# One weight piece converted ahead of the first round, and the loads in another order

## The chip, the cores and the metric

The kernel runs on one core of a Trainium2 chip. The metric is the device time of one execution in microseconds. The engines are TensorE (PE), VectorE (DVE), ScalarE (ACT), GpSimd (POOL) and SyncE (SP). SP only issues DMAs here; ACT issues a few as well. The DMA engines themselves are shared by all queues.

## The reference

An attention block is followed by a feed-forward block. Attention has 8 batches of 8 heads, sequence 576, head dimension 64, in float32:

```
scores = q @ k.T / 8
scores = where(scores >= rowmax(scores) - tau, scores, -1e9)
attn   = exp(scores - rowmax) / (rowsum + 1e-9)
x      = attn @ v            # then heads side by side: 4608 tokens x 512
```

The feed-forward block takes x through `w_in` (512 x 1024), then `h * softmax(h)`, a layer norm scaled by `g_ln`, and `w_out` (1024 x 512). The two weight matrices come as 64-bit floats, so the kernel, which works in float32, has to convert them.

## The kernel before

**Rounds.** The program is written out by a Python loop over rounds (`rnd`), 144 of them (NS), each with one slot of attention. A slot is 128 rows of scores of two heads at once. In each round PE makes the scores (`scores`, L386), DVE takes the row maximum less tau (`maxes`, L407), ACT makes the threshold (`ramp`, L422) and the exponential (`exps`, L431). One round later POOL normalises (`normalise`, L438 to L441) and DVE transposes in blocks of 32 (`blocks`, L453). Two slots make a unit; after the second one, three or four DMAs on SP (`wT<-T`, L462 to L469) move the blocks to where PE needs them. Some three rounds on, PE multiplies by v (`attend_steps`, pv, L494) and ACT keeps the result (xh, L524). The slot numbers and rounds are the same: unit of slots 6 and 7 has its pv in round 10.

The feed-forward work of a block of 128 tokens lies between these: `ff_h` (L557) in two rounds, then maximum (L572), exponential (L581), product (L587), statistics, normalising (L623 on ACT, L628 on DVE), a swap by DMA (L639), a transpose (uT, L649), and `ff_o` (L662) in two rounds. The first `ff_h` is in round 11, the first `ff_o` in round 17.

**The weights.** There are 16 pieces (NW) of 128 x 512: eight of `w_in`, eight of `w_out`. Each is loaded as 512 KB of 64-bit values (`weight_load`, a tile `raw`) and turned into float32 by integer steps:

- `weight_a`: exponent (DVE L253, ACT L258) and mantissa bits (DVE L259)
- `weight_b`: low word and mantissa (DVE L273), sign and exponent (DVE L276)
- `weight_gain`, for `w_out` only: times the gain `gs` (ACT L292)
- `weight_c`: product of the two (POOL L286)
- `weight_d`, for `w_out` only: two DMAs on SP that copy the piece with its halves swapped (`w<-w`, L299)

In round r, piece r has its `weight_b` and piece r + 1 its `weight_a`; `weight_gain`, `weight_c` and `weight_d` of piece r follow in round r + 1. So piece 15 is done in round 16. Each raw piece takes a buffer that belongs to other tiles later: `xh2`, `xh3`, `uT`, `xh1` in turn. The load of piece x + 4 is issued on SP right after `weight_b(x)`, and waits until that is done with the buffer. Pieces 0 to 2 are loaded from ACT's queue.

**The start.** q and k of pair 0 are turned on PE (`turn`, L323), copied to SBUF by ACT and DVE (`keep`, L340 to L344; q is scaled by `scl`, which comes from tau), and pairs 1, 2, 3 follow in rounds 0, 2 and 4 (`whole_pair`). `constants` fills small tiles and makes `scl` from tau. `gains` turns `g_rows` into `gs` in round 3.

**Order.** All of it is in the order of the program on each engine. SP's DMAs too start in program order, so one that waits for a buffer holds up all behind it.

Of the kernel before, what the change touches and what calls it, by code (L numbers as in the profile page):

```python
# [8 lines left out]
F32 = mybir.dt.float32  # L9
I32 = mybir.dt.int32  # L10
U32 = mybir.dt.uint32
I64 = mybir.dt.int64
# [4 lines left out]
P = 128  # L17
# [3 lines left out]
def kernel(  # L21
# [27 lines left out]
    nc = tc.nc  # L49
# [4 lines left out]
    NP = H // 2  # L54
    NPAIR = B * NP
    NC = DFF // P
# [8 lines left out]
    work = ctx.enter_context(tc.tile_pool(name="work", bufs=2))  # L65
# [11 lines left out]
    zero = const.tile([P, 1], F32, name="zero")  # L77
    ntau = const.tile([P, 1], F32, name="ntau")
    scl = const.tile([P, 1], F32, name="scl")
    g_rows = work.tile([NC, P], F32, tag="V", bufs=1, name="g_rows")  # L80
    gs = const.tile([P, NC], F32, name="gs")
    lims = [const.tile([P, 1], F32, name=f"lim{x}") for x in range(2)]

    wide = w_in.dtype == I64
# [4 lines left out]
    NK = S // 64  # L89
# [37 lines left out]
    def load_pair(i, nm, queue=None):  # L127
        raw = loads.tile(
            [P, NK * D], F32, tag="ends" if i == NP - 1 else nm, bufs=BUFS["ends" if i == NP - 1 else nm], name=nm
        )  # L130
        whole_rows[i, nm] = raw.rearrange("p (m d) -> p m d", m=NK)
        (queue or nc.sync).dma_start(out=raw, in_=rows_of[nm][P * i : P * i + P])
# [10 lines left out]
    def load_v(b, hf, parts):  # L143
        d = halves.setdefault((b, hf), {})
        if 0 in parts:
            d["v"] = loads.tile([P, 4, NK, D], F32, tag="v", bufs=3, name="v")
        to = d["v"].rearrange("p h m d -> p h (m d)")
        rows = rows_of["v"][64 * (H * b + 4 * hf) :][0:256]
        for part in parts:
            nc.sync.dma_start(**(  # L150
                dict(
                    out=to.rearrange("p (e o) n -> p o e n", o=2)[:, 0],
                    in_=rows.rearrange("(e r) n -> r e n", e=2),
                ),
                dict(out=to[:, 1], in_=rows[64:192]),
                dict(out=to[ROWS[1], 3], in_=rows[0:64]),
                dict(out=to[ROWS[0], 3], in_=rows[192:256]),
            )[part])
# [66 lines left out]
    def piece(x):  # L225
        if x < 2 * NP:
            c, hf = divmod(x, 2)
            cols = slice(512 * hf, 512 * hf + 512)
            return w_in[P * c : P * c + P, cols], w1[:, c, cols], W_UNIT
        c = x - 2 * NP  # L230
        return w_out[P * c : P * c + P], w2[:, 2 * c], gs[:, c : c + 1]

    NW = 2 * NP + NC
    raws = {}

    def weight_load(x):
        raw = work.tile(
            [P, 512], I64 if wide else F32, tag=("xh2", "xh3", "uT", "xh1")[x % 4 if x < 15 else 0],
            bufs=1, name="raw"
        )  # L240
        queue = nc.scalar if x < 3 else nc.sync
        queue.dma_start(out=raw, in_=piece(x)[0])
        raws[x] = dict(raw=raw)

    def weight_a(x):
        if not wide:
            return
        d = raws[x]
        hi = d["raw"].bitcast(I32).rearrange("p (n two) -> p n two", two=2)[:, :, 1]
        d["em"] = e, m = [  # L250
            work.tile([P, 512], I32, tag=t, bufs=n, name="em") for t, n in (("ob", 2), ("xe", 1))
        ]
        nc.vector.tensor_scalar(  # L253
            out=e, in0=hi, scalar1=20, scalar2=0x7FF,
            op0=ALU.logical_shift_right, op1=ALU.bitwise_and,
        )

        nc.scalar.activation(out=e, in_=e, func=AF.Relu, bias=lims[x >= 2 * NP], scale=8388608.0)  # L258
        nc.vector.tensor_scalar(  # L259
            out=m, in0=hi, scalar1=0xFFFFF, scalar2=0x100000,  # L260
            op0=ALU.bitwise_and, op1=ALU.bitwise_or,
        )

    def weight_b(x):
        d = raws[x]
        _, dst, unit = piece(x)
        if not wide:
            nc.vector.tensor_scalar(out=dst, in0=d["raw"], scalar1=unit, scalar2=None, op0=ALU.mult)
            return
        words = d["raw"].bitcast(I32).rearrange("p (n two) -> p n two", two=2)  # L270
        lo, hi = words[:, :, 0], words[:, :, 1]
        e, m = d["em"]
        nc.vector.scalar_tensor_tensor(  # L273
            out=dst, in0=lo.bitcast(U32), scalar=2.0**-32, in1=m, op0=ALU.mult, op1=ALU.add
        )
        nc.vector.scalar_tensor_tensor(  # L276
            out=e, in0=hi, scalar=-(2**31), in1=e, op0=ALU.bitwise_and, op1=ALU.bitwise_or
        )

    def weight_c(x):  # L280
        d = raws.pop(x)
        if not wide:
            return
        _, dst, _ = piece(x)
        e, _ = d["em"]
        nc.gpsimd.tensor_tensor(out=dst, in0=dst, in1=e.bitcast(F32), op=ALU.mult)  # L286
# [22 lines left out]
    def pair(i):  # L309
        if i not in pairs:  # L310
            qT = heads.tile([P, S], F32, tag="qT", bufs=6, name="qT")
            pairs[i] = dict(
                qT=qT,
                kT=heads.tile([P, S], F32, tag="kT", name="kT"),
                qe=heads.tile([P, ST], F32, tag="qe", name="qe"),
            )
        return pairs[i]
# [18 lines left out]
    def keep(room, i, nm, ms, by_act):  # L336
        of = room[:, 0 : 64 * len(ms)].rearrange("p (m x a) -> p m a x", a=2, x=32)
        to = pair(i)[nm + "T"].rearrange("p (a m x) -> p m a x", a=2, m=NK)[:, ms[0] : ms[-1] + 1]
        if nm == "k":
            (nc.scalar.copy if by_act else nc.vector.tensor_copy)(out=to, in_=of)  # L340
        elif by_act:
            nc.scalar.activation(out=to, in_=of, func=AF.Copy, scale=scl)
        else:
            nc.vector.tensor_scalar(out=to, in0=of, scalar1=scl, scalar2=None, op0=ALU.mult)  # L344
# [385 lines left out]
    for i in range(2 * NP, NPAIR, 2):  # L730
        b, hf = divmod(i // 2, 2)
# [27 lines left out]
            )  # L759

    with tc.manual_schedule():
        nc.scalar.dma_start(out=tau_t, in_=tau.partition_broadcast(P))
        load_pair(0, "q")
        load_pair(0, "k", nc.scalar)
        weight_load(0)
        constants()
        for x in range(1, 3):
            weight_load(x)
        for i in range(1, NP):
            load_pair(i, "q")  # L770
            load_pair(i, "k")
        nc.sync.dma_start(out=g_rows, in_=g_ln.rearrange("(c p) -> c p", p=P))
        tags, tiles = zip(take("tp"), take("tp"))
        turn(tiles[0], 0, "k", range(NK))
        turn(tiles[1], 0, "q", range(4))
        keep(tiles[0], 0, "k", range(5), True)
        keep(tiles[0][:, 320:], 0, "k", range(5, NK), False)
        keep(tiles[1], 0, "q", range(2), True)
        keep(tiles[1][:, 128:], 0, "q", range(2, 4), False)


        pieces = {r: x for x, r in enumerate(range(16))}
        whole = {0: 1, 2: 2, 4: 3}
        for r, hf, parts in ((0, 0, (0,)), (1, 0, (1, 2, 3)), (3, 1, (0,)), (5, 1, (1, 2, 3))):
            load_at[r] = [lambda hf=hf, parts=parts: load_v(0, hf, parts)]

        ready = []
# [8 lines left out]
        while True:  # L796
# [33 lines left out]
            if more:  # L830
                room = 1
                if busy and quarter > 1 and preps and rnd + 4 < first_slot(preps[0][2]):
                    room = 0
                if room and preps and preps[0][0] <= rnd:
                    items = preps.pop(0)[1]
                scores(rnd, items)
                if rnd == 0:
                    turn(tiles[1][:, 256:], 0, "q", range(4, NK))
                    keep(tiles[1][:, 256:], 0, "q", range(4, NK), True)
                    pairs_free += tags  # L840
                idle = quarter == 0 and cur is None and (
                    prev is None or bool(pv_due) and pv_due[0][0] <= rnd
                )
                loose = idle and rnd > NW
                if loose:
                    keeps(rnd, 0)
                    keeps(rnd, 1)
                maxes(rnd, loose)
                ramp(rnd, 0)
                if rnd == 0:  # L850
                    weight_a(0)
                if not loose:
                    keeps(rnd, 0)
                    keeps(rnd, 1)
                ramp(rnd, 1)
                exps(rnd)
# [86 lines left out]
            if rnd in pieces:  # L943
                x = pieces[rnd]
                weight_b(x)
                for y in {0: (3, 4), 11: (), 12: (15,)}.get(x, (x + 4,)):
                    if y < len(pieces):
                        weight_load(y)
                if x + 1 < len(pieces):
                    weight_a(x + 1)  # L950
            if rnd - 1 in pieces:
                weight_d(pieces[rnd - 1])
# [37 lines left out]
```

## Time and profile before

| | |
|---|---|
| median of 3 runs | 861.9 us (860.43 to 862.63) |
| the profiled execution | 862.95 us, span 861.1 us |
| PE busy | 820.3 us, 95% of the span |
| DVE busy | 681.7 us, 79% |
| ACT busy | 571.5 us, 66% |
| POOL busy | 502.0 us, 58% |
| first PE matmul | 6.85 us |
| first L407 on DVE (round 0) | 11.96 us |
| L407 of rounds 5, 10, 11, 17 | 37.53, 62.27, 69.79, 104.79 us |
| DMA moved | 168.54 MB, mean 196 GB/s |

The span runs from the first to the last instruction in the profile; the execution's own time lies some 2 us above it. Busy time is the sum of an engine's instructions, whether or not something waits for them. A round's start is read from its first L407 on DVE.

### The profile page before, as it was taken

Reading aid. Unit: us, or ns where it says so; the run is one execution under the profiler, and the core shown is the slowest. Engines: PE = TensorE matmul, PEld = TensorE weight load, DVE = VectorE, ACT = ScalarE, POOL = GpSimd, SP = SyncE. Lnnn points to the kernel's source line nnn. Section 1 sums busy time; section 2 is a strip of 40 time slices with the busy share of each in tenths; the row PEclk is TensorE's granted clock in tenths of the full one; section 3 lists DMA queues with packets and bytes.
Section 4 is the critical chain, followed back from the end, with each engine's and each line's share of the span. In section 5 each row is a group of like instructions: output and inputs, shape, how many; then the busy total and the mean of one; then the engine's idle time right before and its main releaser. Section 6 shows DMA issues by size and latency. Waiting matters only on the chain.

```text
span 861.1 us, 36103 instructions
## 1 busy us (share of the span) xinstructions
PE 820.3 (95%) x15361; PEld 561.8 (65%) x15361; DVE 681.7 (79%) x1243; ACT 571.5 (66%) x1127; POOL 502.0 (58%) x944
## 2 busy tenths in 40 slices
PE   4769899899999999999999999999999999999997
PEld 3547576677677667777777775555555565556655
DVE  4998978878788888888788887888788888787361
ACT  5887867767677667777677767777777776775121
POOL 2887856656666656565656655565666665555120
PEclk9779999999999999999999999999999999999999
DMA  7999887988878878887878877888788787655312
GB/s 260 242 264 232 213 219 188 227 231 203 224 196 226 197 180 218 209 220 193 212 197 224 209 184 196 219 217 209 189 223 224 203 189 182 159 142 139 69 38 62
DMA packets 75584, 168.54 MB, mean 196 GB/s; under 512 B 11416, under 2 KB 32928, under 8 KB 75424
## 3 DMA queue, kind: packets, MB, share of 16 engines
q1 hardware_dynamic: 74560, 164.25, 75.8%
q8 instruction: 120, 1.97, 1.0%
q10 hardware_dynamic: 864, 2.00, 0.6%
q14 instruction: 40, 0.33, 0.1%
HBM read 46.14 MB, written 9.44 MB: 65 GB/s over the span
## 4 chain that ended last, share of the span: by engine, by line
PE 79%; DMA 7%; DVE 4%; ACT 3%; SPq 3%; issue 2%; POOL 1%; ACTq 0%; DVEq 0%
PE o_ps L662 26%; PE h_ps L557 22%; PE pv L494 14%; PE s_ps L386 14%; DMA wT<-T 5%; PE h_ps L547 3%; ACT w L422 1%; ACT w L431 1%; DVE w L407 1%; DVE T L453 1%; DMA v<-in_v_dram 1%; SPq L464 1%; DMA k<-in_k_dram 1%; DVE w L273 1%; DMA V<-u 0%
## 5 line engine op out<-in xcount | busy, mean ns | idle before, releaser
L662 PE MATMUL o_ps<-w,uT 64*64 64x256 f32 x4608 | 266.5, 376 | 1.7 <-ACT xh L524 0.6
L422 ACT ACTIVATE w<-s_ps,nth 128x576 f32<-128x576 f32 x280 | 196.7, 738 | 103.7 <-DVE nth L407 89.0
L407 DVE CUSTOM_DVE_ANT_0 w<-s_ps,tau_t 128x576 f32<-128x576 f32 x280 | 200.0, 751 | 79.2 <-PE s_ps L386 52.2
L662 PEld LDWEIGHTS o_ps<-w,uT 64*64 64x64 f32 x4608 | 192.3, 133 | 85.5 <-ACT xh L524 12.3
L441 POOL TENSOR_SCALAR w<-w,sm 128x576 f32<-128x576 f32 x288 | 222.6, 785 | 14.3
L453 DVE STREAM_TRANSPOSE T<-w 128x576 f32<-128x576 f32 x288 | 207.7, 755 | 21.5 <-POOL w L441 19.7
L431 ACT ACTIVATE w<-w,ntau 128x576 f32<-128x576 f32 x288 | 219.5, 766 | 0.0
L557 PE MATMUL h_ps<-w,xh 64*64 64x512 f32 x1856 | 217.1, 589 | 0.7 <-issue 0.7
L494 PEld LDWEIGHTS pv<-wT,v 64*64 64x64 f32 x5760 | 168.2, 137 | 46.5 <-issue 22.7
L386 PE MATMUL s_ps<-kT,qT 64*64 64x512 f32 (+1 forms) x2048 | 168.2, 413 | 14.5 <-ACT w L422 13.5
L494 PE MATMUL pv<-wT,v 64*64 64x128 f32 (+1 forms) x5760 | 172.7, 265 | 7.9 <-DMA wT<-T 6.9
L557 PEld LDWEIGHTS h_ps<-w,xh 64*64 64x64 f32 x1856 | 98.9, 133 | 97.3 <-issue 68.0
L438 POOL TENSOR_SCALAR sm<-sm 128x2 f32<-128x2 f32 x144 | 36.4, 253 | 199.1 <-ACT w L431 195.7
L439 POOL TENSOR_TENSOR sm<-sm,mone 128x2 f32<-128x2 f32 x144 | 108.3, 752 | 12.0
L386 PEld LDWEIGHTS s_ps<-kT,qT 64*64 64x64 f32 x2048 | 66.0, 136 | 24.4 <-ACT w L422 17.9
L524 ACT COPY xh<-pv 128x256 f32<-128x256 f32 x64 | 25.4, 397 | 78.9 <-PE pv L494 78.9
L623 ACT ACTIVATE V<-u,nb,rs 128x1024 f32<-128x1024 f32 x36 | 44.7, 1240 | 38.1 <-POOL nb L613 31.9
L649 DVE STREAM_TRANSPOSE uT<-V 128x1024 f32<-128x1024 f32 x36 | 44.2, 1229 | 18.7 <-DMA V<-u 18.6
L431 ACT ACTIVATION_READ_ACCUMULATOR w<-w,ntau 128x1 f32 x288 | 55.3, 192 | 0.0
L587 DVE TENSOR_TENSOR u<-h_ps,u 128x1024 f32<-128x1024 f32 x36 | 42.8, 1190 | 9.9 <-ACT u L581 9.9
L628 DVE TENSOR_SCALAR u<-u,rs,nb 128x1024 f32<-128x1024 f32 x36 | 34.6, 961 | 17.9 <-ACT V L623 17.9
L572 DVE TENSOR_REDUCE hm<-h_ps 128x1 f32<-128x1024 f32 x36 | 42.9, 1192 | 4.9 <-PE h_ps L547 2.7
(75 smaller groups left out, 559.3 us busy)
## 6 DMA issues: line engine op xcount, KB each, us to landing
wT<-T SPq DMA_DIRECT2D x160, 288.0 KB, 6.5
wT<-T SPq DMA_DIRECT2D x64, 576.0 KB, 5.9
v<-in_v_dram SPq DMA_DIRECT2D x16, 576.0 KB, 5.8
V<-u SPq DMA_DIRECT2D x144, 64.0 KB, 3.5
out_dram<-ob SPq DMA_DIRECT2D x71, 128.0 KB, 2.5
q<-in_q_dram SPq DMA_DIRECT2D x28, 288.0 KB, 6.0
k<-in_k_dram SPq DMA_DIRECT2D x27, 288.0 KB, 6.1
qT<-flip SPq DMA_DIRECT2D x48, 144.0 KB, 3.6
```

What stands on the lines that cost most here:

```text
L386: nc.tensor.matmul(out=ps[h][ROWS[y], ks], lhsT=lhsT, rhs=d["kT"][ROWS[h], ks], start=True, stop=True,)
L407: nc.vector.tensor_tensor_reduce(out=w, in0=ps[:, 0:S], in1=(zero if loose else tau_t).to_broadcast([P, S]), scale=1.0, scalar=BIG, op0=AL ...
L422: nc.scalar.activation(out=d["w"][x], in_=d["w"][x] if d["loose"] else d["ps"][x][:, 0:S], func=AF.Prelu, bias=d["nth"][x], scale=-1.0, al ...
L431: nc.scalar.activation(out=w, in_=w, func=AF.Exp, bias=ntau, scale=1.0, accum_out=sm[:, x : x + 1])
L439: nc.gpsimd.tensor_tensor(out=sm, in0=sm, in1=mone, op=ALU.pow)
L441: nc.gpsimd.tensor_scalar(out=w, in0=w, scalar1=sm[:, x : x + 1], scalar2=1.0, op0=ALU.mult, op1=ALU.mult)
L453: nc.vector.transpose(out=T[:, :, r, h, :], in_=w)
L494: nc.tensor.matmul(out=to, lhsT=d["v"][ROWS[u], (h0 + h - u) % 4, m,], rhs=rhs, start=m == 0, stop=m == NK - 1,)
L557: mm = nc.tensor.matmul(out=h[ROWS[y], f], lhsT=x[ROWS[r], c, ROWS[y]], rhs=w1_parts[ROWS[r], c, part ^ r], start=part == 0 and c == 0, st ...
L623: nc.scalar.activation(out=V, in_=u, func=AF.Identity, bias=nb, scale=rs)
L649: nc.vector.transpose(out=uT, in_=d["V"].rearrange("p y (m x) -> p m y x", x=32))
L662: nc.tensor.matmul(out=d["o"][ROWS[z], 512 * (r ^ other) : 512 * (r ^ other) + 256], lhsT=d["uT"][ROWS[r], m].rearrange("p y x -> p (y x)" ...
```

## The change

Piece 0 is loaded, converted and finished (`weight_a`, `weight_b`, `weight_c`) ahead of round 0, and round r then has `weight_b` of piece r + 1. All steps of pieces 1 to 15 so come one round earlier, and piece 15 is done in round 15. Raw pieces have six buffers instead of four (also `u` and `V`; `g_rows` moves from `V` to `xh0`). Six pieces are loaded ahead of round 0, the seventh behind `weight_b(0)`, and piece x + 6 behind `weight_b(x)`; piece 15 is asked for behind piece 12. ACT's queue keeps only k of pair 0 (now first) and tau; all other loads are on SP, in the order in which they are needed, with the first part of v among them. ACT alone makes the first copies of k and q.

```diff
-    g_rows = work.tile([NC, P], F32, tag="V", bufs=1, name="g_rows")
+    g_rows = work.tile([NC, P], F32, tag="xh0", bufs=1, name="g_rows")
...
-    def weight_load(x):
+    RAW = ['xh2', 'xh3', 'uT', 'xh1', 'u', 'V', 'xh2', 'xh3', 'uT', 'xh1', 'u', 'V', 'xh2', 'xh3', 'uT', 'xh2']
+    ASK = {0: [6], 1: [7], 2: [8], 3: [9], 4: [10], 5: [11], 6: [12], 7: [13], 8: [14], 12: [15]}
+
+    def weight_load(x, queue=None):
         raw = work.tile(
-            [P, 512], I64 if wide else F32, tag=("xh2", "xh3", "uT", "xh1")[x % 4 if x < 15 else 0],
+            [P, 512], I64 if wide else F32, tag=RAW[x],
             bufs=1, name="raw"
         )
-        queue = nc.scalar if x < 3 else nc.sync
-        queue.dma_start(out=raw, in_=piece(x)[0])
+        (queue or nc.sync).dma_start(out=raw, in_=piece(x)[0])
...
     with tc.manual_schedule():
+        load_pair(0, "k", nc.scalar)
         nc.scalar.dma_start(out=tau_t, in_=tau.partition_broadcast(P))
-        load_pair(0, "q")
-        load_pair(0, "k", nc.scalar)
-        weight_load(0)
+        load_pair(0, "q", nc.sync)
+        weight_load(0, nc.sync)
+        load_pair(1, "k", nc.sync)
+        load_pair(1, "q", nc.sync)
+        weight_load(1, nc.sync)
+        load_pair(2, "k", nc.sync)
+        load_pair(2, "q", nc.sync)
+        weight_load(2, nc.sync)
+        weight_load(3, nc.sync)
+        load_pair(3, "k", nc.sync)
+        load_pair(3, "q", nc.sync)
+        nc.sync.dma_start(out=g_rows, in_=g_ln.rearrange("(c p) -> c p", p=P))
+        weight_load(4, nc.sync)
+        load_v(0, 0, (0,))
+        weight_load(5, nc.sync)
         constants()
-        for x in range(1, 3):
-            weight_load(x)
-        for i in range(1, NP):
-            load_pair(i, "q")
-            load_pair(i, "k")
-        nc.sync.dma_start(out=g_rows, in_=g_ln.rearrange("(c p) -> c p", p=P))
         tags, tiles = zip(take("tp"), take("tp"))
         turn(tiles[0], 0, "k", range(NK))
         turn(tiles[1], 0, "q", range(4))
-        keep(tiles[0], 0, "k", range(5), True)
-        keep(tiles[0][:, 320:], 0, "k", range(5, NK), False)
-        keep(tiles[1], 0, "q", range(2), True)
-        keep(tiles[1][:, 128:], 0, "q", range(2, 4), False)
-        pieces = {r: x for x, r in enumerate(range(16))}
+        keep(tiles[0], 0, "k", range(NK), True)
+        keep(tiles[1], 0, "q", range(4), True)
+        weight_a(0)
+        weight_b(0)
+        weight_c(0)
+        weight_load(6)
+        pieces = {r: x for r, x in enumerate(range(1, NW))}
         whole = {0: 1, 2: 2, 4: 3}
-        for r, hf, parts in ((0, 0, (0,)), (1, 0, (1, 2, 3)), (3, 1, (0,)), (5, 1, (1, 2, 3))):
+        for r, hf, parts in ((1, 0, (1, 2, 3)), (3, 1, (0,)), (5, 1, (1, 2, 3))):
             load_at[r] = [lambda hf=hf, parts=parts: load_v(0, hf, parts)]
...
                 if rnd == 0:
-                    weight_a(0)
+                    weight_a(1)
...
                 weight_b(x)
-                for y in {0: (3, 4), 11: (), 12: (15,)}.get(x, (x + 4,)):
-                    if y < len(pieces):
-                        weight_load(y)
-                if x + 1 < len(pieces):
+                for y in ASK.get(x, ()):
+                    weight_load(y)
+                if x + 1 < NW:
                     weight_a(x + 1)
```

## The prediction

> **What bounds the kernel now.** I read the page's 40 slices first, to see where TensorE is not full.
>
> ```profile
> PE   4769899899999999999999999999999999999997
> ...
> DVE  4998978878788888888788887888788888787361
> ...
> PEclk9779999999999999999999999999999999999999
> DMA  7999887988878878887878877888788787655312
> ```
>
> A slice is 21.5 us. TensorE (PE) is full from about the fourth slice on; DVE and the DMA engines are full in the second and third, where PE is not and its clock is cut. The change touches the start and rounds 0 to 16 (to about 105 us), so I asked for busy time by stretch (columns: window, length, busy PE, PEld, DVE, ACT, POOL, PE clock, DMA share, GB/s).
>
> ```profile
> 40.00:50.00 10.00, 6.50 (x112) 4.50 (x108) 9.90 (x21) 7.70 (x16) 8.42 (x11) 0.83 1.03 253
> ...
> 60.00:70.00 10.00, 7.72 (x125) 5.96 (x123) 7.43 (x16) 6.65 (x16) 8.67 (x12) 0.74 0.99 259
> ...
> 200.00:400.00 200.00, 198.72 (x3825) 147.42 (x3820) 167.21 (x304) 139.63 (x277) 121.66 (x235) 1.00 0.83 209
> ```
>
> From 20 to 60 us DVE is busy 9.9 of 10 us: it sets the length of rounds 2 to 9, together with DMA engines that have no spare time. From 200 us on PE is busy 99% of the time. The later rounds are the same instructions in both kernels, so I take it that what is won or lost by round 18 stands at the end. Then the chain that ended last, in order of time (start, length, what), at the start and around 60 us:
>
> ```profile
> 1.17 5.55 DMA k<-in_k_dram
> ...
> 6.85 3.05 PE tp L323 x52
> ...
> 10.35 1.59 PE s_ps L386 x15
> ```
> ```profile
> 56.49 8.61 DMA wT<-T
> 65.10 0.04 issue
> 65.14 3.68 PE pv L494 x65
> ```
>
> The kernel starts when the first k lands (6.72). In round 10 PE waits for the turned attention weights of slots 6 and 7, 8.6 us after the issue of their last third. DVE's own timeline (start, length, instruction, idle time before it) shows what that costs:
>
> ```profile
> 66.95 0.41 DVE L259 TENSOR_SCALAR em<-raw 128x512 int32<-128x512 int32 x1
> 69.79 0.76 DVE L407 CUSTOM_DVE_ANT_0 w<-s_ps,tau_t 128x576 f32<-128x576 f32 x1 [2.43 <-PE s_ps L386]
> ```
>
> DVE had finished round 10 at 67.36 and could begin round 11 only at 69.79. Why does the transfer take 8.6 us? The queue ahead of it is full, though it stood empty earlier. The DMA view of the first 25 us (slices of 0.625 us):
>
> ```profile
> DMA  0037448799999999999999970069989930017499
> GB/s 0 0 29 96 162 100 137 273 413 390 426 403 434 387 417 414 398 401 422 383 394 417 406 262 0 0 79 269 236 291 359 402 144 4 0 26 79 157 334 249
> ```
>
> From 5 to 15 us the engines move about 405 GB/s. From 15 to 25 they move 1.64 MB, which at that rate is 4.1 us: 5.9 us of transfer time are lost, because piece 4 waits for piece 0's buffer and everything on SP waits behind it (issue 15.43).
>
> **The change, part by part.**
>
> *Start.* k goes first on ACT's queue, ahead of tau, as the first q does on SP's. That q, issued at 0.72, landed 4.2 us later, at 4.9: one bound for k. The other: k and q share the engines, and 0.59 MB are through at 5.2 by the GB/s row, 5.6 with the same lag to the landing. I take 5.3 between them: PE starts 1.4 us earlier (1.1 to 1.8). [...]
>
> [...]
>
> *All first copies on ACT.* k takes about 0.7 us on ACT (rows of 128x576: 0.63 to 0.72), q about 0.45. k's 36 matmuls end 2.2 us after the landing, q's 16 at 3.05, so q is in place at 3.55; before, ACT's half was done at 3.45 and DVE's at 3.83. No difference.
>
> *Piece 0 ahead of round 0.* Its bytes are the first 1.11 MB: 6.5 us by the row, landed near 7. Four DVE instructions (0.42, 0.42, 0.69, 0.68), one on ACT (L258, 0.72), one on POOL (L286, 1.29). DVE does the first three by 8.5; ACT's step stands behind its copies of k and q, 9.0 to 9.7; DVE's fourth ends at 10.4. Round 0's scores end near 10.6, when DVE can start L407 (before: 11.96). So it is covered by DVE's wait for the first scores, with 0.2 us to spare on DVE and 1.4 us on the landing. Without that cover each us late is a us of start.
>
> *Rounds 0 to 9.* Each still holds one piece's DVE work, so their length stays. The gain multiplication on ACT (L292, 0.71) begins in round 8 instead of 9, where ACT waits 0.47 for DVE: 0 to 0.2 us, taken as nothing.
>
> *Loads.* Before the first wT transfer (issued 25.5 before, 24 now) the queue now carries nine pieces instead of six: 1.57 MB or 3.9 us more, into the 5.9 us that were lost. Between there and the wT of slots 6 and 7 both kernels load six pieces, the same v and three wT sets. If only the bytes count, that wT lands 2.0 us earlier, at 63.1. If the queue is drained when the first wT comes (8.26 MB at 405 GB/s end at 24.1), nothing stands ahead of it any more, and each later set is limited by its own issue: last third issued at 56.49 - 1.4 = 55.1, plus the 5.9 to 6.5 us that wT takes over the whole run, 61.3. I take the middle, 62.2, since no row decides. [...]
>
> *Round 10.* PE is ready at 62.4 - 1.4 = 61.0 and waits until 62.2; pv starts 2.9 us earlier than 65.14, round 11 at 66.9. DVE alone would allow 67.36 - 1.4 = 65.96. So the start's 1.4 us are inside these 2.9, not on top (bounds 2.0 and 3.8).
>
> *Rounds 14 to 16* lose the piece that moved: L253 and L259 in 14, L273 and L276 in 15, L292 and L286 in 16. On the path is ACT's L258 at 92.74, behind which L623 starts at 93.37, while its other input (POOL, nb) ends at 92.76: 0.6 us (0.5 to 1.2, since L292 at 99.27 is also in the chain).
>
> *The last w_out swap* leaves SP one round earlier. PE waits for it once:
>
> ```profile
> 112.19 0.86 PE L662 MATMUL o_ps<-w,uT 64*64 64x256 f32 x10 [0.50 <-DMA w<-w]
> ```
>
> 0.5 us (0 to 1.4: SP issues the next wT 0.9 us late there, behind these loads). Late next: PE itself.
>
> Sum: 2.9 + 0.6 + 0.5 = 4.0 us. The profiled execution took 862.95 (span 861.1), so 858.95; the median, 861.9, becomes 857.9.
>
> **Rivals.**
>
> *The saturated queue swallows it.* For: DMA share 1.0 from 30 to 70 us; any byte put ahead is paid later. Then the wT of slots 6 and 7 lands at 65.1 still, the earlier start is waited away in round 10, and only 0.6 + 0.5 remain: 860.8. Against: the idle time from 15 to 25.
>
> *Slower: three more pieces stand ahead of wT.* If the time from 15 to 25 cannot be won back (piece 4 and v, 1.1 MB, took 5.6 us from issue to landing at an idle queue), the wT of slots 6 and 7 lands later by three pieces: 3.9 us at 405 GB/s, 6.0 at the 263 GB/s seen at 65 us. Round 11 starts that much later, less 1.1: 864.7 to 866.8. It decides against the change once that wT lands after 65.1 + 1.1 + 2.6 = 68.8.
>
> *PE's clock recovers.* pv of slots 6 and 7 took 3.73 us, that of slots 8 and 9 (at 77.42) 2.23; the granted clock is 0.74 from 60 to 70 and 1.00 after. Without the stall pv may run at full clock, 1.5 us shorter; with the landing at 61.3, DVE then bounds round 11 (3.8), and with the upper bounds of the rest (1.2, 1.4): 855.5. [...]
>
> **How the numbers follow.** My forecast (own range 855.5 to 859.3) has 0.47, the clock case 0.10, the swallowed gain 0.22, slower 0.18; 0.03 is for no effect. A measurement of this kernel tells 0.3% (2.6 us) from no change, so faster needs under 859.3: 0.57; same, with the swallowed gain and no effect: 0.25; slower 0.18. The range runs from 854.5, a little below the clock case, to 862.0, over the swallowed gain; most of the slower case is left out.
>
> **What would show it.** Right: first PE matmul near 5.4; first L407 near 10.6; no empty DMA slices between 5 and 23 us; the wait before round 11's L407 under 1 us; L662's wait for w<-w gone. Wrong: wT of slots 6 and 7 landing after 64, or DVE waiting for raw pieces (L253 idle on a DMA).

## The result and the profile after

The changed kernel took 856.97 us (median of 13 runs, 855.38 to 862.38) against 862.29 us before (13 runs, 857.14 to 868.88). The ratio is 0.9946 [0.9927, 0.9966], so 4.7 us less (2.9 to 6.3). The profiled execution took 856.02 us, span 854.0 us; its forecast was 858.95. In the experiments below, two executions lay far outside all others and are left out of the numbers (3023.6 us of e1, its profiled one, and 1435.7 us of the kernel before, beside e1 to e4).

The page's 40 slices of the changed kernel (a slice is now 21.35 us):

```profile
PE   5669899999999999999999999999999999999997
...
DVE  5999868889788888888788878888888888787361
...
PEclk9789999999999999999999999999999999999999
DMA  8998797898888788897878778888788877655212
```

DVE and the DMA engines are busier in the first slice, and PE's row is much as it was. Busy time by stretch says more (window, length, busy PE, PEld, DVE, ACT, POOL, PE clock, DMA share, GB/s):

```profile
40.00:50.00 10.00, 6.50 (x108) 4.52 (x104) 9.91 (x21) 7.70 (x16) 8.29 (x10) 0.83 1.01 274
60.00:70.00 10.00, 7.52 (x138) 5.47 (x136) 9.90 (x21) 8.59 (x19) 9.35 (x13) 1.00 0.76 186
200.00:400.00 200.00, 198.52 (x3828) 148.60 (x3824) 166.40 (x302) 139.50 (x278) 122.46 (x238) 1.00 0.85 210
```

From 60 to 70 us DVE is now busy 9.90 us instead of 7.43, PE's clock is 1.00 instead of 0.74, and the DMA share is 0.76 instead of 0.99. From 200 us on little differs. The first 25 us of the DMA view show the new order of the loads:

```profile
DMA  0037799974379999999999999999999999893999
GB/s 0 0 26 85 229 398 436 275 164 79 88 266 406 431 423 402 406 423 434 406 419 381 388 421 382 397 384 406 399 397 413 418 413 413 321 170 118 269 369 397
```

The empty stretch from 15 to 25 us is gone; a dip at 5 to 7 us (79 GB/s) is new, and one at 22 us (118 GB/s) is left. Around round 11, PE first and then DVE (start, length, instruction, idle time before it):

```profile
61.88 0.44 PE L496 MATMUL pv<-wT,v 64*64 64x128 f32 x4 [1.63 <-DMA wT<-T]
63.17 2.07 PE L496 MATMUL pv<-wT,v 64*64 64x128 f32 x66 [0.85 <-DMA wT<-T]
```
```profile
66.48 0.41 DVE L261 TENSOR_SCALAR em<-raw 128x512 int32<-128x512 int32 x1
66.82 0.74 DVE L409 CUSTOM_DVE_ANT_0 w<-s_ps,tau_t 128x576 f32<-128x576 f32 x1
```

PE still waits for wT of slots 6 and 7, which landed at 63.12. But the 66 multiplications then took 2.07 us, and DVE went from round 10 to round 11 without idle time. At the start the chain no longer begins with k:

```profile
1.17 6.89 DMA tau_t<-in_tau_dram
...
8.09 0.16 DVE scl L205
...
8.34 0.48 ACT qT L344
...
8.87 2.20 PE s_ps L388 x16
```

k landed at 4.83, earlier than either bound; tau landed at 8.07, and q's copy, which needs `scl`, waited 0.52 us for it. The wait of `ff_o` for the last swapped piece is gone: PE's timeline has its 64 multiplications in one piece.

```profile
104.29 3.71 PE L664 MATMUL o_ps<-w,uT 64*64 64x256 f32 x64
```

Of the 6.93 us between the two profiled executions, 3.85 are there when round 29 starts (163.86 against 167.71). Most of the rest belongs to this execution of the kernel before: its round 30 came 7.35 us after round 29, with a wait that the changed kernel's profile lacks (there, 4.44 us). DVE's timeline of the kernel before:

```profile
175.06 0.76 DVE L407 CUSTOM_DVE_ANT_0 w<-s_ps,tau_t 128x576 f32<-128x576 f32 x1 [2.83 <-PE s_ps L386]
```

### The profile page after: what moved, and what is told of

The parts are those of the page before. It is cut to its first block, busy times and chain, and to the rows that moved or that the text cites. A ratio compares the mean times of both kernels' runs of the same rounds, so it can differ in the third digit from the quotient of the medians.

```text
span 854.0 us, 36100 instructions
## 1 busy us (share of the span) xinstructions
PE 817.5 (96%) x15361; PEld 572.4 (67%) x15361; DVE 681.0 (80%) x1241; ACT 571.4 (67%) x1127; POOL 500.9 (59%) x944
## 4 chain that ended last, share of the span: by engine, by line
PE 79%; DMA 7%; DVE 4%; ACT 3%; POOL 3%; issue 2%; SPq 1%; ACTq 0%; DVEq 0%; POOLq 0%
PE o_ps L664 27%; PE h_ps L559 21%; PE s_ps L388 14%; PE pv L496 14%; DMA wT<-T 4%; PE h_ps L549 3%; ACT w L433 1%; ACT w L424 1%; DVE T L455 1%; DVE w L409 1%; POOL w L443 1%; DMA tau_t<-in_tau_dram 1%; DMA v<-in_v_dram 1%; DMA q<-in_q_dram 1%; POOL sm L441 1%
## 5 line engine op out<-in xcount | busy, mean ns | idle before, releaser
L409 DVE CUSTOM_DVE_ANT_0 w<-s_ps,tau_t 128x576 f32<-128x576 f32 x280 | 199.9, 750 | 72.0 <-PE s_ps L388 47.3
L664 PEld LDWEIGHTS o_ps<-w,uT 64*64 64x64 f32 x4608 | 201.3, 133 | 75.9 <-ACT xh L526 12.6
L496 PEld LDWEIGHTS pv<-wT,v 64*64 64x64 f32 x5760 | 165.6, 135 | 42.4 <-issue 21.2
L388 PE MATMUL s_ps<-kT,qT 64*64 64x64 f32 (+1 forms) x2048 | 168.2, 413 | 15.5 <-ACT w L424 12.9
L496 PE MATMUL pv<-wT,v 64*64 64x128 f32 (+1 forms) x5760 | 169.7, 261 | 5.5 <-DMA wT<-T 4.9
L559 PEld LDWEIGHTS h_ps<-w,xh 64*64 64x64 f32 x1856 | 101.8, 133 | 94.4 <-issue 63.1
L583 ACT ACTIVATE u<-h_ps,hm 128x1024 f32<-128x1024 f32 x36 | 40.2, 1116 | 10.4 <-DMA V<-u 5.7
```

Of the source, the lines that this page charges most:

```text
L388: nc.tensor.matmul(out=ps[h][ROWS[y], ks], lhsT=lhsT, rhs=d["kT"][ROWS[h], ks], start=True, stop=True,)
L409: nc.vector.tensor_tensor_reduce(out=w, in0=ps[:, 0:S], in1=(zero if loose else tau_t).to_broadcast([P, S]), scale=1.0, scalar=BIG, op0=AL ...
L496: nc.tensor.matmul(out=to, lhsT=d["v"][ROWS[u], (h0 + h - u) % 4, m,], rhs=rhs, start=m == 0, stop=m == NK - 1,)
L559: mm = nc.tensor.matmul(out=h[ROWS[y], f], lhsT=x[ROWS[r], c, ROWS[y]], rhs=w1_parts[ROWS[r], c, part ^ r], start=part == 0 and c == 0, st ...
L664: nc.tensor.matmul(out=d["o"][ROWS[z], 512 * (r ^ other) : 512 * (r ^ other) + 256], lhsT=d["uT"][ROWS[r], m].rearrange("p y x -> p (y x)" ...
```

## The experiments

**Theories.** Mine: the loads fill the empty stretch, wT of slots 6 and 7 lands earlier, and this is most of the gain; the conversion one round ahead is worth about 1 us; a still earlier start would be waited away at round 11. Rivals: the conversion does most of it; six buffers matter; the pair of profiles only caught one good and one bad execution. Edits are to the changed kernel. The ratios are to the kernel before, run beside each one.

The table gives the first L407 or L409 of some rounds in each profile (us), then the execution's time less the start of round 29. The two rows of means average three profiles of before and two of the changed kernel; each other row is one profile.

| kernel | round 0 | 11 | 19 | 29 | rest | ratio to before |
|---|---|---|---|---|---|---|
| before, mean | 12.29 | 69.66 | 117.97 | 169.49 | 692.8 | 1 |
| changed, mean | 11.13 | 67.46 | 112.11 | 165.18 | 691.9 | 0.9946, 0.9942 |
| e7 loads only | 10.17 | 67.24 | 115.04 | 166.76 | 691.7 | 0.9959 (e1) |
| e2 conversion only | 12.77 | 69.08 | 113.85 | 166.10 | 692.7 | 0.9947 |
| e3 four buffers | 10.76 | 66.29 | 112.70 | 164.92 | 692.5 | 0.9929 |
| e8 tau on POOL | 11.17 | 66.97 | 111.29 | 163.65 | 694.9 | 0.9928 |
| e9 swaps late | 10.62 | 66.02 | 115.17 | 167.25 | 693.6 | 0.9969 |
| e10 tau alone | 10.05 | 65.51 | 109.67 | 162.04 | 693.4 | 0.9938 |
| e11 late loads | 11.05 | 68.59 | 115.51 | 168.06 | 692.1 | 0.9983 |
| e12 late loads, tau alone | 10.03 | 67.34 | 113.28 | 165.47 | 692.4 | 0.9958 |

The rest lies between 690.9 and 694.9 us in all profiles but the first of before (695.2), whatever the variant. So what the change wins is won by round 29, and some 4 us vary from execution to execution behind it.

**The loads alone (e1, e7).** Piece 0 is converted inside round 0 again; loads and buffers stay as changed.

```diff
-        weight_a(0)
-        weight_b(0)
-        weight_c(0)
-        weight_load(6)
-        pieces = {r: x for r, x in enumerate(range(1, NW))}
+        pieces = {r: x for r, x in enumerate(range(NW))}
...
-                    weight_a(1)
+                    weight_a(0)
```

> The changed kernel with piece 0 converted inside round 0 again (piece r in round r, as before), but with the new order of the loads and the six buffers. Queue theory (the gain is made by the DMA queue: the wT transfer of slots 6 and 7 lands earlier): round 11 starts near 66.8 us as in the changed kernel, some 3 us earlier than before; then the 0.6 us of rounds 14 to 16 and the 0.5 us of the w<-w wait are missing: about 858 to 859.5 us. Conversion theory (the gain is made by taking one piece's work out of the rounds): nothing of it is left, 861 to 862.5 us.

Measured: 859.64 us, ratio 0.9959 [0.9936, 0.9981], 3.5 us less than before. The profile read here is e7, the same program:

> The loads-only kernel once more, for a profile of an ordinary execution. Queue theory: round 11 near 66.8 us, as in the changed kernel; rounds 14 to 17 without the 0.6 us, and PE waits 0.5 us for w<-w again. Conversion theory: round 11 at 69 us or later.

Measured: 858.44 us. Round 11 begins at 67.24, as early as in the changed kernel, and the wait for the swapped piece is back (PE's timeline):

```profile
111.36 0.86 PE L664 MATMUL o_ps<-w,uT 64*64 64x256 f32 x10 [2.23 <-DMA w<-w]
```

So the new order of the loads brings round 11 forward without the conversion. It need not be the bytes in the empty stretch that do it. Round 0 began 2.1 us ahead of the mean of before (k landed sooner, so PE began at 4.81 us instead of 6.85, and the scores took 1.21 us instead of 1.59), round 11 2.4 us. SP could issue the last third of wT of slots 6 and 7 that much earlier; the chain of e7 has it as

```profile
54.70 7.83 DMA wT<-T
```

In the three profiles of before it was issued at 56.49, 56.42 and 57.73 and took 8.61, 7.44 and 8.18 us. The earlier issue is most of the earlier landing, and 7.83 us lie among the times of before.

**The conversion alone (e2).** Loads, order and four buffers as before, piece 0 ahead of round 0:

```diff
-    RAW = ['xh2', 'xh3', 'uT', 'xh1', 'u', 'V', 'xh2', 'xh3', 'uT', 'xh1', 'u', 'V', 'xh2', 'xh3', 'uT', 'xh2']
-    ASK = {0: [6], 1: [7], 2: [8], 3: [9], 4: [10], 5: [11], 6: [12], 7: [13], 8: [14], 12: [15]}
+    RAW = ['xh2', 'xh3', 'uT', 'xh1'] * 3 + ['xh2', 'xh3', 'uT', 'xh2']
+    ASK = {**{x: [x + 4] for x in range(1, 11)}, 12: [15]}
...
```

The loads ahead of round 0 are again those of before, in its order and on its queues, except that piece 3 is loaded with them and piece 4 is asked for ahead of round 0. ACT alone still makes the first copies.

> The changed kernel's conversion (piece 0 ahead of round 0, piece r + 1 in round r), but the loads as before: four buffers, pieces 0 to 2 on ACT's queue, tau ahead of k, v in round 0. Queue theory: the empty time of the DMA engines around 15 and 21 us is back, wT of slots 6 and 7 lands at 65 us or later, round 11 starts at 69 to 70 us; only 0.6 and 0.5 us are won later: 861 to 862.5 us. Conversion theory: most of the 5 us stays, 857 to 858.5 us.

Measured: 858.59 us, ratio 0.9947 [0.9928, 0.9967], 4.6 us less. That was missed: by the medians it does nearly as much as the whole change, and e1 (859.64), e2 and the changed kernel beside them (e4, 857.67) are not told apart, as their intervals overlap. Its start is later (12.77; k landed at 6.8 us, much as before, and the scores took 2.20 us instead of 1.59) and its round 11 only 0.6 us earlier than the mean of before, but by round 19 it is 4.1 us ahead. From round 13 to 16 it takes 17.07 us (before: 17.88 to 18.57), and it has no wait for `w<-w`. The last third of wT of slots 6 and 7, issued at 57.18, took 7.50 us with the loads of before, and 7.31 and 7.52 in the changed kernel: that the filled stretch makes this transfer shorter is not shown.

**Four buffers (e3), and the changed kernel again (e4).** e3 keeps order and conversion and drops the two added buffers (RAW and ASK as in e2; pieces 4 and 5 are not loaded ahead).

> The changed kernel with four raw buffers instead of six (piece x + 4 asked for behind piece x), the order of the loads and the conversion as changed. Queue theory: what counts is that the queue does not stand empty ahead of the first wT, less the pieces put ahead; here about 2 us stay empty but two pieces fewer (2.6 us) are ahead of wT of slots 6 and 7, so round 11 starts within 1 us of 66.8 us and the time is 856 to 858 us. Buffer theory (the gain needs the two more buffers): round 11 starts near 69 us, 859.5 to 861.5 us.

> The changed kernel once more, unchanged, as a partner for the three others. In the profiled pair, 3.8 us of 7 were there by round 29 and 2.9 us came in round 30, where the old kernel's PE waited for wT and ran at half clock. If that stall is no part of the change but comes and goes, the median gain is nearer to 4 to 5 us than to 7: 857 us. If it always goes with the change, the gain is 6 to 7 us.

Measured: e3 857.21 us, ratio 0.9929 [0.9909, 0.9949]; e4 857.67 us, 0.9942 [0.9920, 0.9963]. Six buffers are not needed for the gain; wT of slots 6 and 7 landed at 61.57 without them. In e4 it landed at 63.39, yet round 11 began at 68.10, 1.28 us later than in the first profile of the same program. PE's timeline of e4 shows why:

```profile
63.44 3.74 PE L496 MATMUL pv<-wT,v 64*64 64x128 f32 x66 [0.50 <-DMA wT<-T]
```

The same 66 multiplications took 3.74 us here and 2.07 in the first profile: the granted clock was 0.83 from 60 to 70 us in e4, and 1.00 in the other, where it was full from 57.85 us on. DVE then waited 1.14 us for round 11's scores in e4.

**The kernel before, twice more (e5, e6).** No edit.

> The kernel before, one more profile. In its first profile round 30 began 7.35 us after round 29 (a wait for wT of 2.9 us and PE at half clock), in the profiles of three changed kernels 4.4 to 5.0. If that stall belongs to the kernel before, round 30 begins again over 6.5 us after round 29. If it came by chance, it is under 5.5 us here or comes elsewhere. Round 11 should start at 69 to 70.5 us in both cases (queue theory), as wT of slots 6 and 7 stands behind the same transfers.

> The same kernel before, a third profile, for how much rounds 11 and 30 differ between executions. Queue theory: round 11 at 69 to 70.5 us. Round 30: over 6.5 us after round 29 if the stall belongs to this kernel, under 5.5 if not.

Measured: 859.37 and 864.61 us. wT of slots 6 and 7 landed at 63.87 and 65.91 (65.10 in the first profile). Rounds 29 to 30 took 4.45 and 4.44 us: the 7.35 of the first profile came by chance (e8 had 6.39 there). The wait for the swapped piece varies most; PE's timeline of e5, then of e6:

```profile
112.76 0.87 PE L662 MATMUL o_ps<-w,uT 64*64 64x256 f32 x10 [1.62 <-DMA w<-w]
```
```profile
116.28 0.86 PE L662 MATMUL o_ps<-w,uT 64*64 64x256 f32 x10 [3.56 <-DMA w<-w]
```

**tau from POOL's queue (e8).**

```diff
-        nc.scalar.dma_start(out=tau_t, in_=tau.partition_broadcast(P))
+        nc.gpsimd.dma_start(out=tau_t, in_=tau.partition_broadcast(P))
```

> The changed kernel with tau issued from POOL's queue instead of behind k on ACT's. In the changed kernel tau lands at 8.07 us, 3.2 us after k, and the first copy of q waits for it. Queue theory: tau lands before 6.5, round 0 starts at 10.0 us or earlier instead of 11.1, but round 11 keeps to the wT transfer and starts within 0.5 us of the changed kernel (66.3 to 68.1): time within 0.7 us of the changed kernel, 856.5 to 857.5. Start theory (a us of start is a us at the end): round 11 and the end are 1.1 us earlier, 855.5 to 856.2.

Measured: 855.80 us, ratio 0.9928 [0.9905, 0.9951]; tau landed at 8.14 and round 0 began at 11.17. The edit did not bring tau earlier, so it tests nothing of the start, and its ratio overlaps that of the changed kernel.

**The swaps a round later (e9).** As they were before the change, all else as changed.

```diff
-            if rnd - 1 in pieces:
-                weight_d(pieces[rnd - 1])
-                w2_done = pieces[rnd - 1] == NW - 1
+            if rnd - 2 in pieces:
+                weight_d(pieces[rnd - 2])
+                w2_done = pieces[rnd - 2] == NW - 1
```

> The changed kernel with the w<-w swaps of the w_out pieces (L299 to L301, two DMAs each) issued one round later, where the kernel before has them; all else as changed. Swap theory (the wait of ff_o for the last swap, 0.5, 1.6 and 3.6 us in three profiles of the kernel before and none in any with the swap one round earlier, is the largest term after the DMA queue): the wait is back, 0.5 to 3.6 us, and the time 858.5 to 860.5 us, 1 to 3 us over the changed kernel. Small-swap theory (my prediction, 0.5 us): within 0.7 us of the changed kernel, 857 to 858 us.

Measured: 858.34 us, ratio 0.9969 [0.9949, 0.9989], so by the ratios 2.0 to 2.3 us of the gain are gone. The intervals overlap with those of the changed kernel, and 858.34 lies between the two forecasts, so the time alone decides for neither. The wait is back in PE's timeline:

```profile
109.92 1.00 PE L664 MATMUL o_ps<-w,uT 64*64 64x256 f32 x10 [3.06 <-DMA w<-w]
```

All five profiles with late swaps have this wait (0.50, 1.62, 3.56, 2.23, 3.06; mean 2.2 us), and none of the eight with swaps one round earlier. So issuing the swaps a round earlier removes this wait. What of it is left at the end is another matter, taken up below (the last swap).

**tau alone on ACT's queue, first (e10).** k of pair 0 goes first on SP, then q.

```diff
-        load_pair(0, "k", nc.scalar)
         nc.scalar.dma_start(out=tau_t, in_=tau.partition_broadcast(P))
+        load_pair(0, "k", nc.sync)
```

> The changed kernel with tau alone on ACT's queue, k of pair 0 first on SP's and q behind it. If tau lands late because its small packets alternate with those of the SP queue's transfers, it starts with them here and lands by 5.5 us, before k and q are turned; round 0 then starts 0.4 to 0.5 us earlier than 11.1 at the same clock (10.6), near 9.8 if PE has its full clock. Queue theory: nothing of that is left in round 11, which stays within 0.7 us of the other profiles of the changed kernel (66.8 to 68.1), and the time is 856.5 to 857.5 us. Start theory: 0.5 to 1 us earlier at the end.

Measured: 854.96 us (853.29 to 857.97), ratio 0.9938 [0.9918, 0.9959]. DVE's timeline:

```profile
4.70 0.15 DVE L205 TENSOR_SCALAR scl<-tau_t 128x1 f32<-128x1 f32 x1 [4.70 <-DMA tau_t<-in_tau_dram]
...
10.05 0.76 DVE L409 CUSTOM_DVE_ANT_0 w<-s_ps,tau_t 128x576 f32<-128x576 f32 x1 [0.53 <-PE s_ps L388]
...
60.59 0.74 DVE L409 CUSTOM_DVE_ANT_0 w<-s_ps,tau_t 128x576 f32<-128x576 f32 x1
...
65.51 0.74 DVE L409 CUSTOM_DVE_ANT_0 w<-s_ps,tau_t 128x576 f32<-128x576 f32 x1
```

Against the first profile of the changed kernel, round 0 begins 1.06 us earlier, round 11 1.31 and round 18 1.54. My theory's third part falls: the earlier start was not waited away, since wT was also issued earlier (54.50 against 55.81) and landed earlier (61.41 against 63.12). Round 11 then follows round 10 by 4.92 us, as in the changed kernel: DVE's own work. Whether e10 beats the changed kernel as a whole is not shown, as they ran beside different runs and their intervals overlap. The next pair bears on it.

**Fewer pieces in flight (e11), and that with tau alone (e12).** Pieces 9 to 14 are asked for later, three pieces ahead of use.

```diff
-    ASK = {0: [6], 1: [7], 2: [8], 3: [9], 4: [10], 5: [11], 6: [12], 7: [13], 8: [14], 12: [15]}
+    ASK = {0: [6], 1: [7], 2: [8], 6: [9], 7: [10], 8: [11], 9: [12], 10: [13], 11: [14], 12: [15]}
```

> The changed kernel with pieces 9 to 14 asked for later: piece 9 behind piece 6, 10 behind 7, and so on, three pieces ahead instead of six; pieces 0 to 8 as changed. Ahead of the wT transfer of slots 6 and 7 stand then 12 pieces instead of 15. Queue theory: that wT lands at 61 to 62 us instead of 63.1 to 63.4, round 11 starts at 66 to 67 us, up to where DVE ends round 10; time 855.8 to 857.2 us. Against it: a piece comes too late for DVE (L255 waits for a raw piece), or wT of slots 8 and 9 then waits behind pieces 12 to 14 and round 13 is late: 857.5 to 860 us.

> Both edits: the later loads of pieces 9 to 14, and tau alone on ACT's queue. Queue theory: with fewer transfers ahead of wT, the earlier start is no longer lost in round 10; round 11 is 0.5 us earlier than with the later loads alone, time 855 to 856.8 us. If the start does not count, the same time as with the later loads alone.

Measured: e11 859.97 us, ratio 0.9983 [0.9968, 0.9997]; e12 857.64 us, 0.9958 [0.9940, 0.9975]. The idea that fewer bytes ahead bring wT of slots 6 and 7 earlier failed: 62.89 in e11 against 63.12 and 63.39, although DMA share from 50 to 60 us was only 0.80 (0.97 in the changed kernel). wT of slots 8 and 9 landed at 75.22, later than in the changed kernel (71.65 and 72.16), as the case against had it; DVE waited for no raw piece. Then, in e11's timeline of PE,

```profile
62.93 3.89 PE L496 MATMUL pv<-wT,v 64*64 64x128 f32 x66 [1.11 <-DMA wT<-T]
```

so round 11 begins at 68.59, late as in e4: the granted clock was 0.66 from 60 to 70 us. Later it loses more: the waits of DVE from 60 to 110 us (total, times, longest), of e11 and then of the changed kernel:

```profile
DVE w L409 <- PE s_ps L388: 5.2, 3, 3.0
```
```profile
DVE w L409 <- PE s_ps L388: 2.0, 1, 2.0
```

Between e11 and e12 only the places of tau and k differ, on the same chip with 12 runs each: 2.3 us by the medians, with intervals that just overlap, and 1.25 us at round 11. e12 missed its forecast (855 to 856.8), but an earlier start counts. 854.96 us (e10) is the lowest median of all; the ratios of e3 and e8 to the kernel before beside them are lower still (0.9929, 0.9928), so which variant is best is not shown.

## Why the prediction was right, and where it was not

The time came out right (857.9 forecast, 856.97 measured), but in part by luck. One mechanism stands: conversion one round ahead takes out the swap's wait and shortens round 14 (e2, e9). The other, bytes moved into the empty stretch that bring round 11 forward, is not shown: of the 2.2 us that round 11 came earlier by the means, 1.2 were there at round 0 already, and these the prediction had counted as swallowed.

*Start: 1.4 us forecast, 0.85 measured* (11.96 to 11.11; 1.2 by the means). k came sooner than forecast (4.83 against 5.3). What failed on the way is tau: the forecast took no loss for its place behind k, and no row or run shows that. tau needed 6.89 us from issue to landing instead of 4.3 and held q's copy for 0.52 us. Early k and late tau cancelled, so the scores of round 0 began at 8.87 (8.85 by the forecast's 5.3 and 3.55). They then took 2.20 us instead of 1.59, for a reason that was not shown (the trace's records of the clock begin only at 13.5 us, and at 10.5 before), so L409 began at 11.11 instead of 10.6. k landed with q (4.83 and 4.62): from 3 to 3.5 us the engines moved 40 packets of ACT's queue, which carried k, and 41 of SP's, which carried q. That is ahead of the late bound (5.6), since the engines had moved the 0.59 MB by 4.0 us and not by 5.2 (the GB/s rows).

*Copies, piece 0, rounds 0 to 9: nothing forecast.* DVE had piece 0's four steps done at 10.7 and still waited 0.41 for PE (DVE's timeline), so the cover held. Round 1 began 4.81 us after round 0 instead of 4.41, a loss of 0.4 that I did not have. Round 9 took 5.25 or 5.26 us in all nine profiles with the conversion a round ahead and 4.73 to 4.94 in the four others: 0.3 to 0.5 us where "their length stays" had none. DVE's low-word step (L275, L273 before) took 1.06 us there and 0.77 or 0.78 in the four others; why, was not tried. By round 10 only 0.37 of the start was left (0.6 by the means).

*Loads: wT of slots 6 and 7 forecast at 62.2, came at 63.12 and 63.39.* The end by bytes (63.1) had the right number, but not shown to be for its reason. By the means it lands 1.7 us earlier (64.96 to 63.26). Of these, 1.04 are the earlier issue of its last third (56.88 to 55.84), and 0.66 a shorter way from issue to landing (8.08 to 7.42 us), less than the spread of the three profiles of before (7.44 to 8.61). e2, without the new loads, has 7.50. The other end (61.3, a drained queue and 5.9 to 6.5 us from issue to landing) did not come either: it took 7.3 and 7.5.

*Round 10: 2.9 forecast, 2.97 in the pair of profiles, 2.2 by the means.* The first agreement is partly luck. The landing gave 1.98; the other 0.99 are pv at full clock in that execution and not in e4 (granted clock 1.00 and 0.83 from 60 to 70 us). This is the rival of the clock, and it comes and goes from execution to execution: the 66 multiplications took 2.07 us in the changed kernel, e8, e9 and e10, 2.91 in e3, and 3.4 to 3.9 in the eight others (in e6 the trace has 60 of them, in 3.22), all three profiles of before among them. Round 11 came 55.4 to 55.8 us after round 0 in the first five and 56.3 to 57.8 in the eight. Whether the change makes the full clock likelier is not shown. In the records of before the clock is half from 65.16 to 68.57 us, while pv runs from 65.14 on; in those of the changed kernel it is half from 54.44 to 57.85 us and full when pv starts at 63.17. Why these stretches fall where they do, no run shows.

The step that the runs contradict is "the start's 1.4 us are inside these 2.9, not on top". An earlier start moves the issue of wT too and comes through: e10 against the changed kernel has 1.06 us at round 0 and 1.31 at round 11, e12 against e11 1.02 and 1.25. These are single profiles, but with the same time for pv in each pair.

*Rounds 14 to 16: 0.6 forecast, 0.8 measured in the pair, 1.05 by the means* (rounds 13 to 16 take 17.06 us in both profiles of the changed kernel; 17.88, 18.57 and 17.88 before). The steady part is round 14: 5.37 to 5.39 us in all nine profiles with the conversion a round ahead, 5.93 to 6.63 in the four others. Round 15 varies more: 6.00 in the changed kernel, e2 and e10, 6.25 to 6.27 before and in e7, but 6.14 to 8.12 in e3, e8, e9, e11 and e12.

*The last swap: 0.5 forecast, 1.9 by the three profiles of before.* The mechanism was right; the size of the wait was read from one profile that had the smallest of five. But the wait does not all turn into time. In round 20 DVE waits for another swap by DMA (`V<-u`, for `uT`), and it waits longer there where the first wait is gone. DVE's timeline of before, of the changed kernel, and of e9, whose first wait was 3.06 us:

```profile
126.85 1.25 DVE L649 STREAM_TRANSPOSE uT<-V 128x1024 f32<-128x1024 f32 x1 [2.79 <-DMA V<-u]
```
```profile
123.02 1.25 DVE L651 STREAM_TRANSPOSE uT<-V 128x1024 f32<-128x1024 f32 x1 [3.63 <-DMA V<-u]
```
```profile
123.65 1.25 DVE L651 STREAM_TRANSPOSE uT<-V 128x1024 f32<-128x1024 f32 x1 [0.32 <-DMA V<-u]
```

By the means this second wait is 2.0 us before (2.79, 2.22, 0.92) and 4.0 in the changed kernel (3.63, 4.46); over all profiles it is 1.7 in the five that have the first wait and 3.2 in the eight that have not. So the lead of the changed kernel grows from 3.4 us at round 18 to 5.9 at round 19 and is 4.1 at round 22: some 0.7 us are left, close to the 0.5 forecast, for a reason that I did not have.

Added up by the means, the lead is 2.2 us at round 11, 3.4 at round 18, 4.1 at round 22 and 4.3 at round 29, against 4.7 measured (2.9 to 6.3). The two experiments do not add up to the whole: loads alone gave 3.5, conversion alone 4.6, both together 4.7 and 5.0. With intervals of some 2 us to either side, how the gain divides between them stays open.

*Rivals.* The swallowed gain (wT still at 65.1) and the slower case (wT after 68.8) did not come: 63.12. DVE of the changed kernel waits for a raw piece nowhere in rounds 0 to 11.

## What to carry to other kernels

When a transfer lands earlier after loads were moved, take its earlier issue apart from its time between issue and landing: here the first was 1.04 us of 1.70, and the second within the spread of one kernel's profiles. A wait that is removed can come back at the next transfer: of 2.5 us won at the weights' swap, some 0.7 were left three rounds on. Do not size a wait on a DMA from one profile: the wait for the swapped weights was 0.50 us in the one I had and 0.5 to 3.6 us in five. A tiny transfer that is needed soon is worth issuing first; here 512 bytes for tau landed at 4.67 us when issued first of all on ACT's queue, and at 8.07 behind k.

## What the runs showed that I had not expected

- tau's place in its own queue is not what counts: behind k on ACT's queue it took 6.89 us to land, alone on POOL's queue, issued at 1.23, 6.90 (the chain of waits, e8), and 3.9 when issued first of all on ACT's (0.73, landed at 4.67, e10). What differs in e10 is that it was issued half a microsecond sooner, ahead of every other transfer of its queue; which of the two counts was not told apart. In the changed kernel, from 4.5 to 6 us, the DMA engines moved 55 packets of ACT's queue, all under 512 bytes, beside 60 of SP's queue, and tau landed only at 8.07.

```profile
1.23 6.90 DMA tau_t<-in_tau_dram
```

- The same 16 multiplications for round 0 took 1.21 us (e7), 1.59 (before), 1.77 (e10) and 2.20 (the changed kernel); this difference moves the first L409 by up to a microsecond. The trace's records of the clock begin only at 10.5 us before and at 13.5 in the changed kernel, so whether the clock makes the difference was not shown.
- SP's share of a wT set can be long: in the changed kernel its last two parts of slots 6 and 7 took 4.05 us to issue (SP's timeline), in e11 3.15, though fewer loads were under way; yet the landing came only 0.23 us earlier. What holds these issues stays open.

```profile
55.16 4.05 SPq L466 DMA_DIRECT2D wT<-T  x2
```
```profile
55.09 3.15 SPq L466 DMA_DIRECT2D wT<-T  x2
```
